# Strassen-style seven products, two 64-row tiles side by side, for the first two FFN products of two batches, with a new order of all steps

## The chip, the cores and the metric

The kernel runs on one core of one Trainium2 chip. The core has five engines with a queue of their own each: TensorE (PE, matrix products into the accumulator memory PSUM), VectorE (DVE), ScalarE (ACT), GpSimd (POOL), and SyncE (SP), which here only starts DMA transfers. The metric is the time of one execution in microseconds (us), as the device measures it; a profiled execution also has a span, from its first instruction to its last.

## The reference

A linear attention is followed by a feed-forward network (FFN) without a nonlinearity other than a product:

```python
def phi(x):                       # x: batch 4, heads 4, 1088 positions, 32 wide
    a = np.einsum('rd,bhsd->bhsr', S1, x)
    b = np.einsum('rd,bhsd->bhsr', S2, x)
    return np.einsum('bhsi,bhsj->bhsij', a, b).reshape(*x.shape[:-1], r * r)
...
num = np.einsum('bhsf,bhfd->bhsd', q_p, kv)
den = np.einsum('bhsf,bhf->bhs', q_p, z)[..., None] + 1e-06
...
# x: 4352 rows of 128, w1 and w2: 128x1024, w3: 1024x1024, w_out: 1024x128
a = x @ w1
b = x @ w2
h = a * b @ w3
return (h @ w_out).astype(np.float32)
```

All values are float32, S1, S2 and the weights reach the kernel as float64 words.

## The kernel before

**Stages.** The rows of the FFN are cut into nine groups: g0 to g7 have 512 rows each (two per batch), gr has the 256 rows that are left. The attention of a group ends in the tile xT (128 x 512, the row's 128 values down the partitions). The work in front of that (steps named k0 to k3, q0 to q6, qr, s) and the conversion of the weights from float64 words (w0 to w10, with c and m on ACT, j on DVE, a0 and a1 on POOL) is spread over the first two thirds. w3 and w_out are folded into one 1024x128 matrix w3o (f0 to f7).

**The FFN of one group.** For each of eight column blocks c there are four steps: `g.ca` (PE, x @ w1 block, line 1463), `g.cc` (ACT copies the result from PSUM, line 1468), `g.cb` (PE, x @ w2 block, line 1473) and `g.cm` (DVE multiplies the two, line 1479). `g.co` (PE, line 1486) then adds the block's product with w3o into the output bank. After the eighth, `g.oT` (DVE, line 1502) transposes the output and `g.st` has SP store it. Each of these PE steps is a float32 product of a 128x128 weight with 512 columns; the hardware runs it as two passes, each a weight load (LDWEIGHTS, in the profile's row PEld) and a MATMUL.

**Tiles of the PE array.** A product may be given a part of the array: `tile_position` and the sizes choose rows and columns. The kernel does this already for small products: ps_x (line 1423) and ps_ac (line 1310) use sixteen tiles of 32x32, ps_ab (line 665) eight of 64x32, ps_g (line 597) four of 128x32, and ps_x of the second group (line 1235) two of 128x64 with 512 columns each. None uses 64x128.

**Order.** There is no scheduler at run time. The string ORDER names every step once, and each engine executes its instructions in that order; the sets POOL and ACTS say which steps go to POOL or ACT instead of DVE. SLOTS deals out the buffers by hand, in order of use: eight PSUM banks (kind b), 13 tiles of 128x1024 (l), 32 of 128x512 (m) and so on. A step that reuses a buffer waits until its last reader is done. The loads wait further: no more than four large ones (UNDER_WAY) are under way at a time, in the order of SP's queue. `warm` steps multiply zeros while the PE has nothing else at the start.

In q_wide, for batches 2 and 3 (keys q4 and q6, 1024 rows at once), `x` leaves the attention's results in four PSUM banks and the steps `xT0` and `xT1` (line 1434) copy them with ACT into the xT tiles of two groups, g4 and g5, or g6 and g7.

Of the kernel before, what the change touches and what calls it, by code (L numbers as in the profile page):

```python
# [14 lines left out]
I32 = mybir.dt.int32  # L15
# [8 lines left out]
KIND = {"b": "out h kvz t wa wb", "l": "ph kp cv_m cv_c kh pT w3c w3T", "m": "t2 qT q2 s_hl xT ffa ab ay_C oT",  # L24
# [5 lines left out]
        "012345670452704612036071564164527526452430275310436027143627021423516041607354160735647256"  # L30
        "205137204637203512375163025713640271364072365724061562131760314053147531431431040431214201"
        "36034213602714356710243756047356473674671746025673523650247136504316031653416421460414376",
    "k_g": "0101",
    "l": "0123456789abc0127638954b0a12c357a09283b171427619c704a281b7c58307c2c397621530c2ab",
    "m": 
        "0123456789abcdefghijklmnopqrstuv35104297a8c6hdjgefqstko9mi3h6j1avb4s875pdo13a469j4bo21kd2v"
        "ib26c0mj8eshnti4fqba6vg1p5c9ku7r38otlbs6dqg2rhl6fn7gha1amgtvq8org7qrt4hmer1m6gndgs6n85h5m9"
        "360ubvokijtp",
    "q_m": "0101010",
    "raw": "012012020120120",  # L40
    "s": "012345671502364710523460731245630",
    "x": "012021021201",
}

WARM = [29, 2, 2, 9, 3, 2, 2, 3, 2, 1]
# [16 lines left out]
c.zeros c.ident s.four warm0 q0.load v0.zero k0.zero s.zero c.act s.load q0.tr k0.load0 k0.loadr k0.load1 s.words  # L62
k0.max0 k0.max1 c.mask kr0.load k0.tr1 kr0.tr k0.tr0 s.pair s.lead warm1 s.low s.sum s.rest s.T s.P k0.g k0.lead0
q0.max k0.rest0 s.tc warm2 s.R warm3 q1.tr kr0.kT q0.l2 s.Pc s.c q0.l1 k0.kT1 k0.gram0 s.blk s.blkh s.Pm q0.restT s.KS
q0.rm w1.load k0.lead1 warm4 q0.A0 q1.max k0.ab1 kr0.ab q0.C0 k0.abc1 q0.sma q0.sta k0.rest1 k0.kT0 k1.zero k0.kp1
k1.load s.Pp q1.l2 v0.load q0.C0t k0.gram1 k0.gram2 k0.gram3 k0.gram4 k0.Gm k0.Gt k0.Ga v0.loadr k1.loadr k0.ab0
kr1.load w0.load q0.sha k0.Gb k0.T0 w1.m warm5 q1.l1 k1.tr0 warm6 k1.tr1 q0.sla k0.Ta k0.N0 k0.abc0 warm7 k0.Gc w1.c
k0.kp0 q0.sca kr1.tr warm8 k2.zero kr0.abc k2.loadr k1.max k0.T1 k0.kv0 k0.kv3 k0.Na q0.al q0.phi0 k0.Tc kr1.kT
k1.lead0 k0.Nh q1.rm q0.A1 q0.pt0 k0.Tb k0.N1 kr0.kp q0.smy k0.Nb k0.Nf q0.sty q0.shy k0.kv1 k0.kv2 k0.kvr q0.C1
q0.phi1 q0.C1t q0.sly q0.p01 q1.C0 q0.pt1 q0.scy q0.p2 q0.p12 q0.dn q0.de q0.rc k0.kvm q1.load q0.pc0 q0.pc1 w9.load  # L70
k0.kzt k0.kz k2.load w1.j w1.a0 w1.a1 q1.C1 kr1.ab warm9 q1.Ct k1.kT0 q0.x1 q0.x0 k1.kT1 q1.A0 q0.xs0 q0.xs1 q0.xt0
q0.xc0 q0.xc1 k0.kvc q0.xT0 q0.xt1 q0.xT1 k1.ab q1.sm q1.st q1.sh k1.rest0 k0.kqt g0.6a g0.7a w0.m q1.sl w0.c g0.6c
g0.5a g0.4a q2.tr q1.sca q1.al q1.scy k1.gram0 k1.gram1 k1.gram2 k1.gram3 k1.gram4 q1.p01 q1.p2 q2.max q2.l2 w6.load
kh2.load w0.j kr1.abc g0.5c k2.max g0.7b g0.7c q1.p12 q1.dn k1.Gm q1.de s.AR k3.zero g0.6b w0.a0 k1.abt k1.Gt g0.0a
q1.rc g0.4c q1.bs k1.Ga k1.Gb k1.T0 k1.Gc k1.T1 q3.tr g0.7m g0.0c k1.Ta q1.phi g0.2a q1.pt1 k1.Tb k1.Tc k1.N0 k1.N1
k1.Na g0.5b w0.a1 g0.6m k1.Nr q1.pt0 q3.max q1.pc0 q2.l1 g0.1b g0.3a q3.l2 g0.1a g0.2c g0.4b q1.pc1 q1.x g0.1c
k2.lead0 k2.rest0 k2.gram0 k2.gram1 k2.gram2 k2.gram3 k0.kq q3.l1 k1.Nb k2.gram4 q2.rm s.RC g0.4m k2.kT0 k2.kT1 g0.5m
k2.Gm q2.A0 q2.C0 q2.C1 k2.Gt q3.rm g0.3c k2.Ga k2.Gb q2.Ct w9.c w6.m q1.xT g1.5a g1.5c g0.1m q2.At k1.kp0 g1.1a g1.1c
q1.restT k2.ab q2.sm k3.loadr w2.load w2.c k2.abt w9.m q2.st q2.sh q2.sl q3.A0 q3.C0 q3.C1 g0.0b q3.At q2.sc q3.Ct
g1.7b g1.2a q2.p01 q2.al q2.p2 g1.6a g1.4a g1.2c g1.4c k2.Gc q3.sm g0.0m v1.zero v1.load g1.3b g1.7a k1.kp1 q3.st  # L80
v1.loadr k3.load q2.load g1.7c q2.p12 q2.dn q3.sh k1.kv0 k1.kv2 k1.kv3 k1.kv1 k2.T0 k2.T1 k1.kvr q3.sl g1.5b q2.de
q3.sc q3.p01 q3.al q2.rc q2.bs q3.p2 k1.kvc k1.kqt k1.kq v2.zero w5.load k2.Ta k2.Tb g1.3a g1.6c g1.3c w9.j g0.3b
g1.2b w6.c g1.7m q3.p12 q2.phi0 k3.max g1.0a g1.1b kh3.load g1.3m g1.5m g1.2m g1.0c q2.pT0 g1.0b k2.Tc q2.x g0.3m
w9.a1 w5.m q2.xT0 k2.N0 k2.N1 w5.c g0.2b w9.a0 k2.Na w7.load k3.lead0 w2.j q3.dn g2.7a g2.7c w7.m w7.c k3.kT1 q4.tr
q3.de g1.1m g1.0m g2.2a g1.4b g2.4a g2.5a g2.5c w3.load k3.rest0 w5.j g1.4m k3.gram0 k3.gram1 k3.gram2 k3.gram3
k3.gram4 w6.j k3.Gm k3.Gt q3.rc k3.Ga k3.kT0 q3.bs k3.Gb g2.3a w5.a1 g2.2c w2.m q2.restT q4.max w7.j g2.7b g1.6b g2.6a
k3.Gc g2.1a g2.3c q4.l2 g2.4c w3.m g2.1c g2.6c g2.0a g2.0c k2.Nr g0.2m g1.6m g2.7m q3.phi0 kr1.kp q3.pT0 w2.a0 w2.a1
w6.a1 w6.a0 f6.t g2.5b g2.3b g2.3m g2.4b g2.0b k3.T0 k3.T1 g2.5m k2.Nb g2.4m g2.0m v2.load q3.x k3.ab k3.Ta k3.abt
f6.m q4.l1 q3.xT0 g3.2a g3.2c w3.c q4.rm q3.load g3.4a f6.o g3.0a g3.0c k3.Tb v3.zero f3.t f3.m f3.o k3.kp1 w5.a0 f2.t
k2.kp1 w3.j w3.a1 w4.load k3.Tc q4.A0 q4.C0 q4.C1 k3.N0 k3.N1 f2.m f2.o g3.4c w3.a0 w7.a0 w4.c w4.m q4.Ct q4.At w4.j  # L90
w4.a1 w7.a1 f0.t g2.2b q6.tr k0.Nr w10.load w10.m w10.c g2.2m f4.t g3.7a g3.0b g3.1a g3.6a g3.0m f0.m f0.o g2.6b w4.a0
q6.max w10.j g2.6m g3.1b v3.load k3.Na k3.Nr w8.load g3.5a g2.0o q3.restT k3.Nb k2.kp0 f4.m w8.c f4.o k3.kp0 f1.t
g3.6b q6.l2 g3.7c g3.5c g3.6c g3.6m g2.1b g2.4o g2.1m g3.3a g1.0o q6.l1 q4.sm q6.rm g3.7b g3.7m g3.4b g3.1c g3.1m
g3.4m f1.m k2.kv0 k2.kv3 v2.loadr k2.kv1 k2.kv2 k2.kvr k3.kv0 w8.m f1.o k3.kv1 k3.kv3 v3.loadr k3.kv2 k2.kvc k3.kvr
q6.A0 q6.C0 q6.C1 q4.st q6.At q6.Ct q4.sh g3.3c g0.0o g0.1o g1.1o g3.0o g1.6o k2.kqt w8.j w8.a0 w8.a1 f5.t g1.3o g0.2o
g1.4o g0.6o g0.3o qr.max g3.4o f5.m w10.a0 q4.sl q4.sc q4.p01 w10.a1 q4.al q4.p2 g2.6o k2.kq f5.o g1.5o g1.2o g3.3b
q4.p12 f7.t q6.sm g3.3m g3.2b g3.2m q4.dn qr.l2 qr.l1 qr.rm f7.m f7.o g3.3o k3.kvc k3.kqt k3.kq g3.1o g1.7o g3.6o
# [23 lines left out]
def make_steps(ctx, tc, q, k, v, S1, S2, moe_w1, moe_w2, moe_w3, moe_w_out, out):  # L121
# [1330 lines left out]
    def ffn(g, n, dst, halves=1):  # L1452
        w = n // halves
        for c in range(NC):
# [26 lines left out]
            if g != "r":  # L1481
                @step(f"g{g}.{c}o")
                def _(c=c):
                    if c == 0:
                        o_ps[g] = ps("out", [128, 512], "ps_o")
# [103 lines left out]
```

## Time and profile before

| | us |
|---|---|
| three runs | 252.36, 253.60, 256.84 |
| median | 253.60 |
| profiled execution: time | 253.12 |
| profiled execution: span | 251.3 |
| PE busy in the span | 245.4 |
| DVE busy | 151.1 |
| ACT busy | 104.7 |
| POOL busy | 87.2 |

The profile lists groups of instructions by line of the kernel with their number, their busy time together and the mean of one in ns. A MATMUL's own duration holds its way through the array, which overlaps the next one's start, so the distance from one start to the next is what counts; the chain of waits shows it, as it books each piece of time once. The granted TensorE clock is 1.0 all through. The DMA engines are busy for the first 100 us or so and then nearly idle but for the stores.

### The profile page before, as it was taken

The numbers are of one execution on the slowest core, as the hardware profiler recorded it, in microseconds if no ns is written. First come the engines' busy times: TensorE is split into PE (matmuls) and PEld (weight loads), VectorE is DVE, ScalarE is ACT, GpSimd is POOL, SyncE is SP. The second block draws the span as 40 slices with busy tenths as digits, with TensorE's granted clock in tenths as the row PEclk, the third lists the DMA queues.
The fourth block names the chain that finished last, engine by engine and source line by source line (L and its number), as shares of the span: only waits on it lengthen the run. The fifth ranks groups of instructions, "written<-read, shape, count | busy, mean of one in ns | idle before, by whom it ended". The sixth has DMA issues, their size and how long they took to land.

```text
span 251.3 us, 6192 instructions
## 1 busy us (share of the span) xinstructions
PE 245.4 (98%) x2582; PEld 136.8 (54%) x2582; DVE 151.1 (60%) x322; ACT 104.7 (42%) x210; POOL 87.2 (35%) x112
## 2 busy tenths in 40 slices
PE   8999989999999999999999999999999999999994
PEld 6887544655554676657466444454444445654554
DVE  2698997999799966674539557463523262332320
ACT  2999946755787337464011103433134112210000
POOL 4533966456649886620662550000010000000000
PEclk9999999999999999999999999999999999999999
DMA  7597988586788965000000000025000004000133
GB/s 203 170 244 223 247 183 185 126 261 174 170 196 227 230 178 113 0 4 3 0 3 0 3 0 0 1 36 92 0 0 0 3 4 80 0 3 0 21 63 63
DMA packets 32075, 22.02 MB, mean 88 GB/s; under 512 B 21296, under 2 KB 26672, under 8 KB 32048
## 3 DMA queue, kind: packets, MB, share of 16 engines
q1 hardware_dynamic: 31360, 21.05, 34.5%
q10 hardware_dynamic: 688, 0.59, 0.7%
q8 instruction: 20, 0.33, 0.6%
q14 instruction: 7, 0.06, 0.1%
HBM read 19.40 MB, written 2.23 MB: 86 GB/s over the span
## 4 chain that ended last, share of the span: by engine, by line
PE 88%; DMA 7%; SPq 2%; ACT 1%; DVE 0%; issue 0%
PE b_ps L1473 23%; PE ps_o L1486 22%; PE a_ps L1463 22%; PE ps_w3o L472 6%; DMA k<-in_k_dram 3%; PE idle_ps L220 3%; PE ps_x L1423 2%; PE ps_ac L1310 2%; DMA raw<-in_moe_w_dram 2%; PE ps_kv L707 2%; DMA kr<-in_k_dram 1%; PE ps_g L597 1%; PE ps_or L1493 1%; SPq L531 1%; ACT k_abs L172 0%; PE ps_N L850 0%
## 5 line engine op out<-in xcount | busy, mean ns | idle before, releaser
L1479 DVE TENSOR_TENSOR ab<-ffa,b_ps 128x512 f32<-128x512 f32 (+1 forms) x72 | 45.2, 647 | 53.9 <-PE b_ps L1473 26.6
L1468 ACT COPY ffa<-a_ps 128x512 f32<-128x512 f32 (+1 forms) x72 | 38.7, 567 | 78.1 <-PE a_ps L1463 70.9
L1463 PE MATMUL a_ps<-xT,w 128*128 128x512 f32 (+1 forms) x144 | 66.2, 574 | 0.4 <-DVE kabt L683 0.4
L1473 PE MATMUL b_ps<-xT,w 128*128 128x512 f32 (+1 forms) x144 | 66.3, 573 | 0.0
L1486 PE MATMUL ps_o<-ab,w3o 128*128 128x512 f32 x128 | 60.0, 594 | 0.0
L1463 PEld LDWEIGHTS a_ps<-xT,w 128*128 128x128 f32 x144 | 26.5, 190 | 30.8 <-issue 22.6
L1473 PEld LDWEIGHTS b_ps<-xT,w 128*128 128x128 f32 x144 | 26.5, 190 | 28.5 <-issue 23.1
L1486 PEld LDWEIGHTS ps_o<-ab,w3o 128*128 128x128 f32 x128 | 23.8, 190 | 25.1 <-issue 23.9
L439 POOL TENSOR_TENSOR w3c<-w3c,cv_m 128x512 int32<-128x512 int32 x16 | 20.1, 1270 | 15.8 <-DVE w3c L433 13.3
L472 PEld LDWEIGHTS ps_w3o<-wo,w3T 128*128 128x128 f32 x128 | 15.4, 192 | 3.3 <-issue 2.0
L1405 POOL TENSOR_TENSOR ph<-s_al,s_bs 128x1024 f32<-128x1024 f32 (+1 forms) x5 | 9.9, 1975 | 19.5 <-DVE s_bs L1395 13.2
L472 PE MATMUL ps_w3o<-wo,w3T 128*128 128x128 f32 x128 | 15.8, 276 | 0.0
L420 ACT ACTIVATE cv_m<-raw 128x1024 int32<-128x1024 uint32 x11 | 12.9, 1182 | 4.0 <-PE ps_w3o L472 3.5
L466 DVE STREAM_TRANSPOSE w3T<-w3c 128x1024 f32<-128x1024 f32 x8 | 9.9, 1240 | 6.7 <-POOL w3c L439 4.5
L228 ACT ACTIVATE cv_c<-raw 128x1024 f32<-128x1024 f32 x11 | 13.0, 1179 | 0.0
L615 POOL TENSOR_TENSOR kp<-kabt 128x1024 f32<-128x1024 f32 x6 | 12.5, 2084 | 1.0 <-DVE kabt L683 1.0
L589 POOL TENSOR_TENSOR kk<-k,kk 128x1152 f32<-128x1152 f32 (+1 forms) x4 | 9.7, 2434 | 5.6 <-DVE kk L179 4.4
L220 PE MATMUL idle_ps<-zeros 128*128 128x256 bf16 x55 | 10.6, 349 | 1.0 <-DVE zeros L194 1.0
L476 ACT COPY w3o<-ps_w3o 128x128 f32<-128x128 f32 x8 | 2.1, 262 | 20.2 <-PE ps_w3o L472 20.2
L1434 ACT COPY xT<-ps_x 128x128 f32<-128x128 f32 (+2 forms) x20 | 4.7, 322 | 13.4 <-PE ps_x L1423 13.4
L1372 POOL TENSOR_TENSOR s_pr<-s_al,s_hl 128x128 f32<-128x128 f32 (+2 forms) x4 | 2.4, 589 | 20.6 <-DVE s_al L1362 20.6
L1413 DVE STREAM_TRANSPOSE pT<-ph 128x1024 f32<-128x1024 f32 (+1 forms) x7 | 8.2, 1167 | 1.0 <-POOL ph L1405 0.8
(260 smaller groups left out, 300.4 us busy)
## 6 DMA issues: line engine op xcount, KB each, us to landing
raw<-in_moe_w_dram SPq DMA_DIRECT2D x32, 256.0 KB, 5.1
qh<-in_q_dram SPq DMA_DIRECT2D x4, 544.0 KB, 3.9
out_dram<-oT SPq DMA_DIRECT2D x33, 64.0 KB, 1.9
raw<-in_moe_w_dram SPq DMA_DIRECT2D x4, 512.0 KB, 5.4
k<-in_k_dram SPq DMA_DIRECT2D x3, 512.0 KB, 5.1
v<-in_v_dram SPq DMA_DIRECT2D x2, 512.0 KB, 4.1
kh<-in_k_dram SPq DMA_DIRECT2D x8, 128.0 KB, 3.2
raw<-in_moe_w_out_dram SPq DMA_DIRECT2D x4, 256.0 KB, 5.7
```

The costliest lines, as they stand in the source:

```text
L220: pe.matmul(t, zeros, bview(zeros, [[0, 2], [1, 128]]), start=True, stop=True)
L228: act.activation(dst, hi.bitcast(F32), ACT.Prelu, scale=2.0 ** -112, alpha=-2.0 ** 32)
L420: act.mul(x["m"], words(0).bitcast(U32), 2.0 ** -29)
L439: pool.tensor_tensor(d, d, x["m"][:, i * 512:(i + 1) * 512], ALU.add)
L466: dve.transpose(w3T[ko].rearrange("p s (i r) -> p s i r", r=32), bview(w3c[ko], [[32, NC], [256, 4], [1, 32]]))
L472: pe.matmul(t["o"], w3T[ko][:, c], wo[:, c], start=c == 0, stop=c == NC - 1)
L615: eng.tensor_mul(dst, bview(av, [list(av.ap[1]), list(av.ap[2]), [0, r]]), bview(bv, [list(bv.ap[1]), [0, r], list(bv.ap[2])]))
L1463: pe.matmul(x["a"][:, :w], w_of(0, c), xT[g][:, c0:c0 + w], start=True, stop=True)
L1468: act.copy(x["s"][:, :w], x["a"][:, :w])
L1473: pe.matmul(x["b"][:, :w], w_of(1, c), xT[g][:, c0:c0 + w], start=True, stop=True)
L1479: dve.tensor_mul(ab_sb[g, c][:, c0:c0 + w], x["s"][:, :w], x["b"][:, :w])
L1486: pe.matmul(o_ps[g], w3o[:, c], ab_sb[g, c], start=c == 0, stop=c == NC - 1)
```

## The change

The two first FFN products of batches 2 and 3 are computed as block products. With x of one batch cut into two row halves (groups g and g+1) and two halves of 64 of the inner dimension, and a weight cut likewise into two halves of 64 rows and two halves of 512 columns, a 2x2 by 2x2 block product takes seven products of blocks in place of eight (the Winograd form of Strassen's method). Each is a 64x128 tile with 512 columns. The product of w1 (u=0, "a") sits in rows 0 to 63 of the array, that of w2 (u=1, "b") in rows 64 to 127; they are separate steps in ORDER.

```diff
+    def seven(g):
+        mv = {}
+        own = {1: (0, 0), 2: (0, 1), 4: (1, 1)}
+        ...
+        @step(f"h{g}.s1")
+        def _():
+            mv[5] = sb("xd", [128, 512], name="xd")
+            on(f"h{g}.s1").tensor_add(mv[5], xd[g, 1][0], xd[g, 1][1])
+        ...
+        for i in range(NC // 2):
+            both = {}
+            for u in range(2):
+                ...
+                def prod(j, bank, new, i=i, u=u, x=x, n=n):
+                    @step(n(j))
+                    def _():
+                        if new:
+                            x[bank] = ps("h", [128, 512], "ps_" + bank)
+                        pe.matmul(x[bank], stat(j, u)[:, i * 128:(i + 1) * 128], rows(j, u), start=new, stop=True,
+                                  tile_position=(u * 64, 0), skip_group_check=True)
+                def take(y, bank, k, n=n, x=x):
+                    ...
+                        act.copy(x[k], x[bank])
+                def plus(y, bank, k, n=n, x=x):
+                    ...
+                        dve.tensor_add(x[k], x[k], x[bank])
+                prod(1, "X", True)
+                take("c", "X", 11)
+                prod(5, "Y", True)
+                take("d", "Y", 22)
+                prod(6, "X", False)
+                take("e", "X", 12)
+                prod(3, "Y", False)
+                plus("f", "Y", 12)
+                prod(7, "X", False)
+                plus("g", "X", 22)
+                prod(2, "Z", True)
+                plus("h", "Z", 11)
+                prod(4, "X", False)
+                if u == 0:
+                    take("i", "X", 21)
+            for k, (t, c) in {11: (0, 0), 12: (0, 4), 22: (1, 4)}.items():
+                @step(f"h{g}.{i}m{k}")
+                ...
+                    on(f"h{g}.{i}m{k}").tensor_mul(both[0][k], both[0][k], both[1][k])
+            @step(f"h{g}.{i}m21")
+            ...
+                dve.tensor_mul(both[0][21], both[0][21], both[1]["X"])
     def ffn(g, n, dst, halves=1):
         w = n // halves
-        for c in range(NC):
+        whole = g != "r" and g >= 4
+        for c in range(0 if whole else NC):
```

`s1` to `s4` are four sums or differences of this size. So a bank X takes four products one after the other, and an engine reads it after each: ACT, ACT, DVE, and last ACT (for u=0) or DVE. For each i (four per pair of groups) that makes 14 products, 7 copies by ACT, 6 sums by DVE and 4 multiplications; 13 of the 32 multiplications are in the set POOL. The products with w3o take the blocks in the order 0, 4, 1, 5, 2, 6, 3, 7.

What goes with it:

- `v.s`, `v.t` (ACT, two copies of 64x512) and `v.1` to `v.4` (POOL, eight subtractions of 64x512) make the sums of weight blocks.
- `xT0` to `xT3` of q4 and q6 write the tiles xd, split by inner half: each step four copies of 64x256, on ACT for xT0 and xT2, on DVE for xT1 and xT3.
- In q4 and q6 the rows of x are scaled by powers of two: `na`, `nb` (peaks, DVE), `nm`, `nn` (multiplications), `nr`, `ne` (small, DVE), and `ns` (17 small instructions, POOL), which makes the factors that undo it. `oS` multiplies the transposed output by them (POOL for g4 and g6, DVE for g5 and g7).

```diff
+            if whole:
+                @step(f"g{g}.oS")
+                def _():
+                    y = oT[0].rearrange("p (t d) -> p t d", d=32)
+                    on(f"g{g}.oS").tensor_mul(y, y, bview(scale[g], [[1, 16], [0, 32]]))
```

ORDER, SLOTS, POOL and WARM are new throughout. The PE's order from the first of the new products to the end is, with a and b for a 64x128 product of either kind, x for a ps_x of 32x32 tiles, O for a product with w3o (line 1486 before), g and r for gr's products:

```
abbaaba x abbaababaab x babaababbaabbbaaababab OOO abbaababbaababababab
OO g OOOOOO g OO g OOO g bababbaaabbbaaabbbaababab g O g
baabbbaaababbbaaabbababaabab OOO gggg OOOO g OOOOOOOO ggggg rrrrrrrrrrrrrrrr
```

From the first FFN product on, the shape of the tiles changes 38 times along PE's queue before, and 48 times after. In SP's queue the load of w0 (half of w1 and w2) stands behind w1, k1, v0, kr1 before; after, it stands behind these and the loads of kh2 (four), k1's rest and q1:

```diff
-k1.load s.Pp q1.l2 v0.load q0.C0t k0.gram1 k0.gram2 k0.gram3 k0.gram4 k0.Gm k0.Gt k0.Ga v0.loadr k1.loadr k0.ab0
-kr1.load w0.load q0.sha k0.Gb k0.T0 w1.m warm5 q1.l1 k1.tr0 warm6 k1.tr1 q0.sla k0.Ta k0.N0 k0.abc0 warm7 k0.Gc w1.c
...
+k0.kv0 k0.kv3 k0.T1 kr0.kp k0.Na kr1.tr q0.al k0.Nh k0.Tb q1.l1 k2.loadr kh2.load k0.Tc k1.kT1 k1.kT0 q0.phi0 q1.A0
+q0.A1 q0.smy k0.N1 k0.Nb k0.kv1 k0.kv2 k0.kvr q0.phi1 k0.kvm k0.Nf q0.pt0 q0.sty q0.shy q0.C1 k0.kvc k1.loadr q0.pc0
+q1.rm k0.kzt q0.pt1 k1.max kr1.kT s.AR q0.p01 q0.sly q0.C1t q0.scy q1.load q0.p2 q0.p12 k0.kz w0.load k2.load k0.kqt
...
+kr1.ab q1.Ct k1.abt k1.lead0 w0.c w1.a0 s.RC k1.rest0 w0.j q3.tr g0.4a g0.7a g0.5a w0.m g0.6a k1.gram0 k1.gram1
+k1.gram2 k1.gram3 k1.gram4 w6.load w9.load w2.load g0.5c w1.a1 q1.sm q1.st q2.tr k2.kT1 g0.4b q3.max g0.7c k1.Gm k1.Gt
+q1.sh g0.6c k0.kq k2.max w0.a1 w0.a0 g0.4c g0.2a g0.1b k1.Ga q1.sl q1.scy q1.sca k1.Gb g0.4m k1.Gc kr1.abc k1.T0
```

274 lines of the change are left out of this document (195 added, 79 removed).

## The prediction

> **What bounds the kernel now.** I read the page's busy table first, then the windows for three stages, then the chain of waits, and last the groups of lines.
>
> ```profile
> span 251.3 us, 6192 instructions
> PE 245.4 (98%) x2582; PEld 136.8 (54%) x2582; DVE 151.1 (60%) x322; ACT 104.7 (42%) x210; POOL 87.2 (35%) x112
> ```
>
> ```profile
> 26.80:40.00 13.20, 11.93 (x209) 6.20 (x208) 11.36 (x30) 7.76 (x17) 10.19 (x10) 1.00 0.86 197
> 40.00:150.00 110.00, 109.98 (x1411) 61.88 (x1410) 83.42 (x163) 52.98 (x96) 62.52 (x55) 1.00 0.42 104
> 150.00:248.20 98.20, 97.92 (x460) 48.68 (x458) 37.69 (x71) 22.55 (x49) 2.35 (x3) 1.00 0.13 22
> ```
>
> The window columns are the stretch, then busy time of PE, PEld, DVE, ACT and POOL, the granted clock, the DMA share and GB/s. From the first FFN product (26.8 us) to the last one PE has no gap worth naming except 1.27 us before 40. In the last stage, where the change is, DVE is busy for 37.69 of 98.20 us, ACT for 22.55, POOL for 2.35. But busy is not yet full: what one pass of a product costs is read from the chain of waits (start, length, what).
>
> ```profile
> 41.43 1.72 PE a_ps L1463 x4
> ...
> 44.08 1.01 PE ps_x L1235 x4
> 45.08 1.82 PE ps_g L597 x88
> ...
> 48.08 1.91 PE a_ps L1463 x4
> ...
> 122.85 5.15 PE ps_o L1486 x12
> ...
> 244.57 3.36 PE ps_or L1493 x30
> 247.96 0.29 DVE oT L1513
> ```
>
> Twelve passes of 512 columns take 5.15 us, 0.429 each, and four take 1.72. The same four take 1.91 behind the ps_ac piece, which uses small tiles: a change of tile shape costs 0.19. So the end is PE's sum of passes, plus a price for each change of shape, plus the tail of stores behind 248.25.
>
> **The products.** Removed are 4 groups x 8 blocks x 2 products x 2 passes = 128 passes x 0.429 = 54.9 us. Added are 2 pairs x 4 blocks x 2 sides x 7 = 112 products of 64x128 tiles. Whether two of them run at once, no row of 64x128 shows. The nearest is ps_x at line 1235: two tiles of 128x64 side by side, four passes of the same 512 columns in 1.01 us where the full array needs 1.72. Two rounds of 0.429 are 0.86; the 0.15 left over is one entry and exit. I take it that two row tiles overlap in the same way. How many rounds that makes I counted on PE's order: a change of shape lets both sides run out, so each of the six stretches lasts as long as its longer side, 4, 6, 11, 10, 13 and 14 products, 58 in all where 56 would be ideal. That holds if PE may start a b that stands behind two or three a's. If it may not, the same walk gives 62.
>
> ```profile
> L597 PE MATMUL ps_g<-kk 128*32 128x64 f32 x288 | 7.5, 224 | 0.3 <-POOL kk L589 0.2
> L597 PE MATMUL ps_g<-k,kk 128*32 128x32 f32 x288 | 7.2, 194 | 0.0
> ```
>
> ps_g decides for 58: it puts two products in a row on each of its four tiles. At 0.429 us for 512 columns, 288 passes of 64 columns and 288 of 32 stream for 15.4 + 7.7 = 23 us, and all of it is done in about 7.5, three tiles at a time. PE does look past a busy tile. So 58 x 2 x 0.429 = 49.8 us; saved: **5.1 us** (bounds 1.7 and 5.1).
>
> The loads of weights double to two for each round.
>
> ```profile
> L1486 PEld LDWEIGHTS ps_o<-ab,w3o 128*128 128x128 f32 x128 | 23.8, 190 | 25.1 <-issue 23.9
> ```
>
> A load takes 190 ns, and passes on one array still follow every 0.429 us, so a load is hidden behind the pass before it on the same rows. The Trainium skill (TensorE: Matmul & The Clock Gate, Part 3, The mechanism) says that a load overlaps matmuls under way only where the row group differs, which speaks against this change: each side would wait for its own loads. The trace differs, by the 0.429, and I go by the trace.
>
> **Changes of shape.** 48 in place of 38 on PE's queue from the first FFN product on: 10 x 0.19 = **1.9 us** lost. From the 0.15 of an entry and exit together it would be 0.8; I take 0.19, since it is of a full-width load.
>
> **Work on the other engines.**
>
> ```profile
> L1479 DVE TENSOR_TENSOR ab<-ffa,b_ps 128x512 f32<-128x512 f32 (+1 forms) x72 | 45.2, 647 | 53.9 <-PE b_ps L1473 26.6
> L1468 ACT COPY ffa<-a_ps 128x512 f32<-128x512 f32 (+1 forms) x72 | 38.7, 567 | 78.1 <-PE a_ps L1463 70.9
> L439 POOL TENSOR_TENSOR w3c<-w3c,cv_m 128x512 int32<-128x512 int32 x16 | 20.1, 1270 | 15.8 <-DVE w3c L433 13.3
> ```
>
> ```profile
> L1434 ACT COPY xT<-ps_x x20: 267/296/402, 66.6 to 206.7; 128x128 f32<-128x128 f32 x8, 128x256 f32<-128x256 f32 x8, 128x64 f32<-128x64 f32 x4
> L1502 DVE STREAM_TRANSPOSE oT<-ps_o x8: 698/714/718, 148.9 to 244.6; 128x512 f32<-128x512 f32 x8
> ```
>
> DVE in the last stage: 37.69, plus 48 sums x 0.647 = 31.1, minus 13 multiplications that go to POOL (8.4), plus eight copies of q6 at about 0.296 (2.4), plus three s and two oS at 0.647 (3.2): 66 of some 95 us. ACT: 22.55 + 24 more copies x 0.567 + 2.4 = 39. POOL: 2.35 + 13 x 1.27 + two oS and five s at 1.27 = 28, and the small copies of `ns` (priced at 0.3 each from the shortest xT copies, 32 of them 10). All lie beside PE. The v and n steps of q4 come before 150 us, where POOL has 47 of 110 us free; eight subtractions at 1.27 are 10. The densest stretch is the one of 13 products: PE 13 x 0.857 = 11.1 us, DVE 12 sums, a multiplication, an oS, gr.5m (at most 0.647) and a transpose, 15 x 0.647 + 0.714 = 10.4. That is 94%, and there the cover is thin: DVE's queue runs in order, so a late sum holds all sums behind it, and the PE product that reuses its bank.
>
> This is the new kind of wait: a bank X gets four products, and between two of them an ACT copy (0.567) or a DVE sum (0.647) must end. Eight banks and two sides leave other products to run meanwhile. In the kernel before such waits are small:
>
> ```profile
> PEld a_ps L1463 <- ACT ffa L1468: 2.0, 5, 0.6
> PEld ps_g L597 <- POOL kk L589: 1.9, 2, 1.1
> ...
> PEld a_ps L1463 <- POOL w L439: 1.2, 1, 1.2
> ```
>
> Five waits of weight loads for the copy make 2.0 us, most of it hidden by the pass under way. Bounds for the new waits: nothing, or one DVE sum for each of the eight blocks, 8 x 0.647 = 5.2. I take 0.6, near the lower end, as that row is.
>
> **What is moved.** At the start w0's load goes behind q1's, which waited for PE:
>
> ```profile
> 15.30 1.08 SPq L395 DMA_DIRECT2D raw<-in_moe_w_dram  x2
> ...
> 21.50 0.33 SPq L913 DMA_DIRECT2D qh<-in_q_dram  x1
> ```
>
> ```profile
> 19.59 1.25 ACT L176 ACTIVATE kk<-k,k_g 128x1152 f32<-128x1152 f32 x1
> ...
> 26.84 3.66 PE L1463 MATMUL a_ps<-xT,w 128*128 128x512 f32 x8
> ```
>
> ```profile
> raw<-in_moe_w_dram SPq DMA_DIRECT2D x4, 512.0 KB, 5.4
> ...
> L420 ACT ACTIVATE cv_m<-raw 128x1024 int32<-128x1024 uint32 x11 | 12.9, 1182 | 4.0 <-PE ps_w3o L472 3.5
> L228 ACT ACTIVATE cv_c<-raw 128x1024 f32<-128x1024 f32 x11 | 13.0, 1179 | 0.0
> ```
>
> If q1 is still issued at 21.5, w0 follows at 21.9 (15.30 before), lands 5.4 later at 27.3, and needs two ACT conversions (2.4) and two POOL additions (2.5): 32.2, or 34.7 if ACT's k1.lead0, now in front of it, delays it by two passes of 1.25, as the row of the same operation shows. PE has other work to about 33: behind 26.84 four products of w1 (3.4), k1's gram (1.8, from the ps_g piece of the chain) and one b (0.86). The 1.2 us wait for w in the row above becomes 0 to 1.7; I take no difference. The rest of the head is only shuffled; the first product's time may shift by a microsecond either way, which I leave to the range.
>
> At the end DVE has, behind g7's last block, two transposes, an oS and six gr multiplications: 2.1 + 6 x 0.647 at most = 6.0, PE meanwhile five gr products (2.1) and ps_or (3.36): 0 to 0.5, taken as nothing. The last store follows as before.
>
> **Sum.** The profiled execution took 253.12, its span 251.3 with 1.8 around it; the median of the three runs, 253.6, lies 0.5 above. 253.1 - 5.1 + 1.9 + 0.6 = **250.5 us**.
>
> **Rivals.**
> - *The new order also recovers the head.* If the waits for kk (1.9) and w (1.2) go and no new ones come: 249.9 - 3.1 = 246.8. For it: these are the only idle stretches left, and the order is new throughout. Against it: both hang on loads and conversions of which w0's comes later now.
> - *The banks' chain becomes the bound.* One sum's length lost per block: 249.9 + 5.2 = 255.1. For it: 94% DVE in one stretch. Against it: 69% over the stage. It decides once DVE's share in a stretch passes PE's.
> - *Side by side costs each pair what line 1235 cost once (slower).* If the 0.15 above the two rounds is not entry and exit but paid by every pair of products: 58 x 0.15 = 8.7, 249.9 + 8.7 = 258.6. It beats the saving from 0.055 per pair on. Against it: the 0.15 is smaller than one change of shape. The same page of the Trainium skill (Part 3, Measured speedup) gives 3.07 for four row tiles instead of 4; by that factor 49.8 would be 65 us, an estimate, and the result 265. No run here shows row tiles of that size.
> - *Loads do not hide in a half array.* Each side pays 58 x 2 x 0.190 = 22.0: 271.9. This is what the overlap rule would do; against it stands 0.429 per pass with 0.190 loads.
>
> **Chances.** Forecast 0.59 (its own range 248.8 with the cheap changes of shape and no waits, to 252.0), head 0.16, chain 0.13, pairs 0.09, loads 0.03. The range 246.8 to 258.6 reaches from the head to the pairs. Two per cent, about what a measurement tells, is 248.1 and 258.2. Faster: 0.16 + 0.02 from the forecast's edge = 0.18. Slower: 0.09 + 0.03 + 0.02 from a worse chain = 0.14. Within: 0.68.
>
> **What would show it.** Two rows of 64x128 passes that start within a few ns and follow on each side every 0.43 us, PE about 98% busy, and a stage from the first new product to the last ps_or some 3 us shorter. A spacing of 0.5 or 0.62 shows the third or fourth rival. Waits of PE or PEld for the sums or copies of the new banks above 2 us show the second. A first FFN product far from 26.8 us shows that the head, not the products, made the difference.

## The result, and the profile after

| | before | after |
|---|---|---|
| runs shown (us) | 252.36, 253.05, 253.60, 256.84 | 259.58, 261.18, 262.10, 262.60 |
| median | 253.32 | 261.64 |
| ratio after/before, 95% interval | | 1.033, 1.0245 to 1.0416 |
| profiled execution: time, span | 253.12, 251.3 | 259.58, 257.8 |
| first FFN product starts | 26.84 | 26.74 |
| last product of ps_or starts | 247.65 | 253.68 |

The changed kernel is 3.3% slower. The profiled execution of it is its fastest: there the granted TensorE clock was 1.0 throughout, in the three others it averaged 0.983 to 0.990, and they took 1.6 to 3.0 us more; the last section comes back to this. Some executions of a kernel take over 1.5% longer than its fastest; the medians in this document hold all executions, the ratios leave these out.

The busy table of the page and the windows (stretch, then busy time of PE, PEld, DVE, ACT and POOL, granted clock, DMA share, GB/s) answer to those of before; the windows are cut at the first new product, 157.7 us:

```profile
span 257.8 us, 6599 instructions
...
PE 246.1 (95%) x2681; PEld 139.6 (54%) x2681; DVE 187.5 (73%) x388; ACT 123.9 (48%) x244; POOL 126.7 (49%) x178
```

```profile
26.80:40.00 13.20, 10.43 (x170) 5.25 (x170) 9.37 (x25) 8.67 (x18) 5.35 (x8) 1.00 0.88 227
40.00:150.00 110.00, 107.05 (x1503) 61.21 (x1502) 95.34 (x196) 58.08 (x104) 75.08 (x80) 1.00 0.43 105
150.00:157.70 7.70, 7.70 (x20) 3.21 (x18) 7.53 (x10) 0.00 (x0) 2.99 (x4) 1.00 0.00 1
157.70:254.30 96.60, 95.21 (x481) 49.15 (x480) 57.67 (x101) 37.48 (x78) 30.34 (x40) 1.00 0.14 23
```

PE, which was idle for 1.27 us between 26.8 and 40 and for 0.02 from there to 150, is now idle for 2.77 and 2.95. That is in front of the new products. PE's waits (engine, line, what it waited for: total, times, longest) say for what:

```profile
PE ps_g L608 <- issue: 2.5, 2, 2.0
PE b_ps L1664 <- ACT ffa L1659: 1.4, 1, 1.4
...
PE a_ps L1654 <- POOL w L450: 0.9, 1, 0.9
PE ps_ac L1314 <- POOL AR L903: 0.8, 1, 0.8
PE ps_X L1601 <- ACT hc L1608: 0.6, 1, 0.6
```

The second and third are w0. The chain of waits there (start, length, what) shows that the load took 8.8 us, where 5.4 was the median before; ACT's conversion, in order, held the copies ffa behind it, and POOL's additions came last:

```profile
22.65 8.77 DMA raw<-in_moe_w_dram
...
31.50 1.16 ACT cv_c L239
32.66 1.05 ACT cv_m L431
...
33.78 2.50 POOL w L450 x2
...
36.33 0.70 PE a_ps L1654
```

The fourth is a small product of batch 3 that waits for `k3.Nr` on POOL, in whose queue `v.1` (two subtractions) now stands in front. The first and longest wait has no releaser: "issue" is time in which the engine waited for nothing that the profile shows. PE's timeline (start, length, what, count, and in brackets the idle time before) shows it in the middle of the small products of k2's gram:

```profile
46.79 0.22 PE L608 MATMUL ps_g<-kk 128*32 128x64 f32 x1
46.80 0.23 PE L608 MATMUL ps_g<-k,kk 128*32 128x32 f32 x2
49.07 0.19 PE L608 MATMUL ps_g<-k,kk 128*32 128x32 f32 x1 [2.05 <-issue]
```

All products around it are of one step on data that is there. What arrives just then is seen in the page's table of DMA queues (packets, MB, share): PE's instructions themselves.

```profile
q8 instruction: 21, 0.34, 0.6%
```

PE has 5424 records here (weight loads, passes, sequencer), so one of the 21 packets of 16 KB goes with some 258 of them; in the kernel before it is 20 packets for 5209. In the trace one of these packets starts at 46.65 and takes 1.10 us; 1.33 us after it landed PE goes on. The shorter stand of ps_g, 0.67 us at 31.3, ends 1.46 us after another. Counted in order from 0, PE goes on there with instructions 1729 and 1217, which are 512 apart, two chunks of 256. That made the theory that most experiments below test: **PE had run out of instructions.**

The new products do run two side by side. The chain in a stretch that has as many a's as b's:

```profile
183.35 1.06 PE ps_X L1601 x4
184.41 0.42 PE ps_Z L1601
184.84 0.01 PE ps_X L1601
184.84 0.42 PE ps_Z L1601
185.26 0.01 PE ps_X L1601
185.27 0.86 PE ps_Y L1601 x4
```

Two passes of 512 columns start 0.01 us apart or less, and the next two follow 0.42 later; four take 0.86, half of 1.72 on the full array. The stretches as a whole, windows again:

```profile
157.74:161.55 3.81, 3.81 (x15) 1.37 (x14) 3.34 (x9) 2.28 (x5) 2.57 (x3) 1.00 0.40 62
163.90:169.86 5.96, 5.88 (x28) 2.70 (x23) 5.50 (x12) 5.57 (x13) 5.07 (x15) 1.00 0.28 46
170.64:180.51 9.87, 9.87 (x50) 4.92 (x44) 7.74 (x13) 5.71 (x13) 4.09 (x5) 1.00 0.01 2
183.28:192.15 8.87, 8.87 (x42) 4.30 (x41) 5.94 (x9) 3.91 (x7) 3.77 (x3) 1.00 0.00 0
205.23:217.09 11.86, 11.86 (x52) 6.67 (x51) 8.63 (x15) 6.05 (x11) 1.64 (x2) 1.00 0.21 35
219.31:232.80 13.49, 12.92 (x55) 5.96 (x54) 5.74 (x9) 7.26 (x14) 5.04 (x5) 1.00 0.05 8
sum 53.86, PE 53.20 PEld 25.92 DVE 36.91 ACT 30.78 POOL 22.19; mean PE 8.87 PEld 4.32 DVE 6.15 ACT 5.13 POOL 3.70
```

53.86 us, where 49.8 were forecast. If each pass counts its columns at full rate (0.429 us for 512 on the whole array), PE's passes from the first FFN product on are some 205 us before and 198 after: (128 - 112) x 0.429 = 6.9 were taken off the array. But in the stage behind 150 us, 3.3 us were lost beside the passes before, and 9.8 after. So this stage ends up with some 0.4 us gained, and the stages in front lose some 6.5. Behind the last product of ps_or 0.4 us more are lost (4.1 us to the end of the span, 3.7 before).

### The profile page after: what moved, and what is told of

It is laid out like the page before. It is cut to its first block, busy times and chain, and to the rows that moved or that the text cites. A ratio compares the mean times of both kernels' runs of the same rounds, so it can differ in the third digit from the quotient of the medians.

```text
span 257.8 us, 6599 instructions
## 1 busy us (share of the span) xinstructions
PE 246.1 (95%) x2681; PEld 139.6 (54%) x2681; DVE 187.5 (73%) x388; ACT 123.9 (48%) x244; POOL 126.7 (49%) x178
## 4 chain that ended last, share of the span: by engine, by line
PE 80%; DVE 5%; POOL 5%; DMA 3%; ACT 2%; issue 2%; SPq 0%; ACTq 0%; DVEq 0%; POOLq 0%
PE ps_o L1689 21%; PE ps_X L1601 11%; PE b_ps L1664 10%; PE a_ps L1654 10%; PE ps_Y L1601 6%; PE idle_ps L231 4%; DMA raw<-in_moe_w_dram 3%; PE ps_Z L1601 3%; PE ps_g L608 2%; PE ps_x L1476 2%; PE ps_ac L1323 2%; PE ps_w3o L483 2%; PE ps_or L1678 1%; PE ps_kv L718 1%; ACT xd L1489 1%
## 5 line engine op out<-in xcount | busy, mean ns | idle before, releaser
L1601 PE MATMUL ps_X<-xd,wv 64*128 64x512 f32 x112 | 41.0, 605 | 0.6 <-ACT hc L1608 0.6
L1608 ACT COPY hc<-ps_X 128x512 f32<-128x512 f32 x40 | 22.5, 591 | 37.1 <-PE ps_X L1601 33.3
L1659 ACT COPY ffa<-a_ps 128x512 f32<-128x512 f32 (+1 forms) x40 | 21.1, 548 | 34.8 <-PE a_ps L1654 32.5
L1664 PE MATMUL b_ps<-xT,w 128*128 128x512 f32 (+1 forms) x80 | 36.4, 559 | 1.5 <-ACT ffa L1659 1.4
L1654 PE MATMUL a_ps<-xT,w 128*128 128x512 f32 (+1 forms) x80 | 35.6, 557 | 0.9 <-POOL w L450 0.9
L1635 POOL TENSOR_TENSOR hc<-hc 128x512 f32<-128x512 f32 x13 | 16.2, 1273 | 29.6 <-DVE hc L1613 29.6
L1689 PE MATMUL ps_o<-ab,w3o 128*128 128x512 f32 x64 | 29.4, 597 | 0.0
L1689 PE MATMUL ps_o<-hc,w3o 128*128 128x512 f32 x64 | 29.3, 599 | 0.0
L1670 DVE TENSOR_TENSOR ab<-ffa,b_ps 128x512 f32<-128x512 f32 (+1 forms) x40 | 23.9, 619 | 7.5 <-PE b_ps L1664 7.5
L1601 PE MATMUL ps_Y<-xd,wv 64*128 64x512 f32 x48 | 20.6, 603 | 0.1
```

The costliest lines, as they stand in the source:

```text
L1601: pe.matmul(x[bank], stat(j, u)[:, i * 128:(i + 1) * 128], rows(j, u), start=new, stop=True, tile_position=(u * 64, 0), skip_group_check=True)
L1608: act.copy(x[k], x[bank])
L1635: on(f"h{g}.{i}m{k}").tensor_mul(both[0][k], both[0][k], both[1][k])
L1654: pe.matmul(x["a"][:, :w], w_of(0, c), xT[g][:, c0:c0 + w], start=True, stop=True)
L1659: act.copy(x["s"][:, :w], x["a"][:, :w])
L1664: pe.matmul(x["b"][:, :w], w_of(1, c), xT[g][:, c0:c0 + w], start=True, stop=True)
```

## Experiments

The theory "order" says that the loss comes from what the new order of all steps does in front of the new products; the rival "products", that the products and their side work cost more than they save. Ratios are to the kernel before in the same runs, since its median moved between 253.5 and 255.9 from one set of runs to the next. Where steps were moved, buffers were dealt out anew only where needed.

**Half the change each.** head_of_before:

```diff
 ORDER, POOL, WARM
-    the changed kernel's, up to q1.x
+    those of the kernel before, up to k2.kT1 (46 us); then what is left, in the changed kernel's order
```

> The changed kernel with the steps of the first 46 us in the order, the POOL set and the warm-up of the kernel before; everything behind them, the seven products too, in the changed kernel's order. Theory 'order' (the loss of the changed kernel comes mostly from idle stretches of PE that the new order makes in front of the new products: 2.9 us more lost between 26.7 and 50 us, 3.5 more from 50 to 150): the 2.9 come back, 261.6 - 2.9 = 258.7. Rival 'products' (the seven products and their side work cost more than they save, and idle stretches in front only move): no gain, 261 to 262.

Measured 262.96 us, 1.029 (1.017 to 1.041): no gain. It settles nothing: at the seam a DVE step of q3 runs for 4.6 us, until 53 us, beside two multiplications of POOL (1.9 us each; in the changed kernel's trace the same step takes 2.35), PE stands 2.3 us for what is behind it on DVE, and the granted clock is at half behind that (shown in the last section).

eight_in_new_order:

```diff
-    xd, v, n, s steps; 2 x 4 x 14 products of 64x128
+    g4 to g7 with 64 ordinary products, from q4.bs on in the order of the kernel before
```

> The eight ordinary products in place of the seven: the changed kernel's order up to q4.bs (127 us there) without the v and n steps, then the rest in the order of the kernel before. Theory 'order': the losses of the head and the middle stay without the seven products, 253.3 + 2.9 + 0.8 + about 1.5 = 258.5. Rival 'products': about 253.3, as the kernel before.

Measured 263.72, 1.036 (1.028 to 1.045). Without a single new product the new order is as slow as the changed kernel. That speaks for "order", though one stretch of 2.7 us at 129 us, behind work of POOL, belongs to the seam, and the clock was at half for 6.8 us from 34.6. PE stood at instructions 1217 and 1729 here too, 1.23 and 1.40 us.

**The waits that the trace names.** w0_early and w0_early_v1_late:

```diff
-q1.load q0.p2 q0.p12 k0.kz w0.load k2.load
+q1.load q0.p2 q0.p12 k0.kz k2.load
-kr1.load kr0.abc
+kr1.load w0.load kr0.abc
```

> The changed kernel with the one step w0.load moved forward, to right behind kr1.load, as in the kernel before. If the late landing of w0 makes PE's gaps at 32.8 (1.55 us) and 35.3 (1.07 us): 261.6 - 2.6 = 259.0, and those two gaps are gone in the profile; the gaps at 31.3 (0.65) and 46.9 (2.2), which end with no releaser, stay. Rival: w0's conversion is late for another reason (ACT's queue in front of it), no change, 261.6.

```diff
-qr.max v.1 k2.kp0
+qr.max k2.kp0
-k3.Nr q4.p2
+k3.Nr v.1 q4.p2
```

> As w0_early, and the step v.1 (POOL, two subtractions of 64x512) moved behind k3.Nr in POOL's queue. If the gap of 0.98 us at 115.4 (a product waits for AR, whose step stood behind v.1) is real loss: 1.0 less than w0_early, about 258.0. Rival: the q4 chain behind it is what the stage waits for, same as w0_early.

Measured 260.64, 1.026 (1.018 to 1.034), and 259.56, 1.022 (1.015 to 1.029). The gaps named do go, but less than their length is won with the first: its first FFN product starts at 30.0 us, since PE stood 2.5 us at instruction 705 and then ran at half clock from 22 to 25 us. The stands at ps_g stayed, both in w0_early and the longer one in w0_early_v1_late, 2.30 us.

**Where PE's instructions are cut.** after_phase and before_phase add instructions to the warm-up at the very start and leave everything else alone:

```diff
+            for _ in range(26 if name == "warm0" else 0):      # before_phase: 77
+                pe.matmul(t[:, :16], zeros, zeros[:, :16], start=True, stop=True)
-WARM = [30, ...                                              # before_phase: 29
+WARM = [24, ...                                              # before_phase: 10
```

> The changed kernel with the first warm-up of 30 products of zeros (256 columns) replaced by 24 of them and 26 of 16 columns: about as long, but 40 PE instructions more (a weight load and a pass each). Theory 'instruction fetch': PE's instructions come in chunks of 256 (16 KB, one fetch of the instruction queue each), and PE stands where a chunk runs out before the next has come; in three kernels of this order it stood at the same instructions, the 1217th and the 1729th, 512 apart. 40 more in front move the chunks' borders out of the small products of ps_g: the two stretches at 31.3 (0.65) and 46.9 us (2.2) go, 261.6 - 2.9 = 258.7, and less if the granted clock then also stays at 1.0. Rival (memory or semaphores hold ps_g, or the fetch is late whatever the border): both stretches stay at ps_g, 261 to 262.

> The kernel before with the first warm-up of 29 products of zeros replaced by 10 of them and 77 of 16 columns, 116 PE instructions more, nothing else. Theory 'instruction fetch': from the times of PE's instructions, a chunk of 256 needs about 4.3 us, and with this shift the chunks' borders fall so that ps_g at 32 and 47 us, and chunks at 117 and 170 us, come up to 2.8, 2.7, 2.4 and 1.7 us late: 4 to 9 us slower, 258 to 262. Rival: where the borders lie does not matter, within 1 us of the kernel before, 253 to 254.5.

Measured: after_phase 257.23, 1.0155 (1.0115 to 1.0196), from 1.033, and neither stand is left in its trace. (Its wait for the copies ffa is shorter too, 0.3 us for 1.4.) before_phase 260.85, 1.032 (1.026 to 1.039): with 116 more instructions of zeros the kernel before is as slow as the changed one. The theory had the places wrong, and that the size came out was luck: of the 6.8 us that the profiled execution lost, 4.2 are stands, 1.24, 1.30 and 1.64 us in other small products, at instructions 705, 961 and 1985. Much of the rest lies in the head, where the nine warm-up products of `warm3` take 2.10 us for 1.16 before.

repaired and seven_on_before were the next try at both theories:

```diff
 repaired: w0_early_v1_late
+with the warm-up of after_phase
 seven_on_before: head_of_before
-with its seam at k2.kT1
+with its seam at q6.A0 (116 us)
```

> The changed kernel with all three repairs: w0.load early, v.1 behind k3.Nr, and the 40 instructions of after_phase. If the losses in front of the new products are these: 259.6 (w0_early_v1_late) - 2.3 (the one stretch left at ps_g there) - 1 to 2 of granted clock = 255 to 257. Rival: the losses only move, 259 or more.

> The kernel before's order, POOL set and warm-up up to q6.A0 (116 us there), then the rest in the changed kernel's order with the seven products and the scaling. Theory 'order' (the seven products by themselves save little but do save): the stage behind 150 us loses 0.75 us less than before, so 253.3 - 0.75 + up to 1.5 for the seam = 252.5 to 254. Rival 'products': 258 or more.

Measured 258.13, 1.022 (1.015 to 1.030), and 273.19, 1.077 (1.070 to 1.084). The repairs do not add up: repaired has only 1.4 us of idle PE from its first FFN product to the last of ps_or, but that starts at 30.6 us, behind a wait of 2.6 us and 3.4 us at half clock: in its chain of waits w0's load (7.9 us) now stands in front of one of k (2.4 us), and ACT's work on that k in front of the copies that lead to the product. seven_on_before is a miss that tells nothing of the products: its seam puts a fold's transpose behind work of DVE and POOL, and its longest waits are there.

```profile
PE ps_w3o L478 <- DVE w3T L472: 6.5, 1, 6.5
PE b_ps L1659 <- ACT ffa L1654: 2.5, 1, 2.5
PE b_ps L1659 <- DVE ay_C L1335: 2.2, 1, 2.2
```

**A control, POOL, the scaling, and the order of the new products.** before_phase_256 puts 147 for the 77 small products. after_phase_v1 is after_phase with `v.1` behind `k3.Nr`. no_scaling drops 18 steps from it. balanced has the 366 steps from the first new product to the end in an order that a search with a small model of that stage found.

> As before_phase, but with 147 instead of 77 small products of zeros in the first warm-up: 256 PE instructions more than the kernel before in place of 116, one whole chunk, so that every border lies where it lay. Theory 'instruction fetch': the loss of before_phase goes, 253 to 255. Rival (the small products warm PE up worse than the 29 full ones, and that is what made before_phase slow): about as before_phase, 259 to 261.

> after_phase with v.1 moved behind k3.Nr on POOL (w0.load stays late). If the stretch of 0.95 us at 112 (a product waits for AR) is real loss: 257.2 - 0.95 = 256.3. Rival: the chain behind it sets the pace, no change, 257.2.

> after_phase_v1 without the scaling by powers of two (the steps na, nb, nm, nr, ne, nn, ns of q4 and q6 and oS of g4 to g7 are left out). The prediction costed this work at nothing, since it lies beside PE: then 256.3 as after_phase_v1, within 0.5. Rival: the steps between bs and phi0 of q4 and q6 lengthen the chain that the new products wait for, and DVE and POOL lack the time in the last stage: 1 to 2.5 us less, 254 to 255.

> after_phase_v1 with all steps from the first 64x128 product to the end in another order (same steps, buffers dealt out anew): products of the two halves alternate more evenly, and the sums and copies come sooner. A model of that stage, which gives the measured times of after_phase within 1 us, puts the end 5.6 us earlier. Theory (the stage of the new products loses 9.6 us, of which about 3 to waits and one-sided rounds, because of its order, not by nature): 256.3 minus 3 to 5, 251.5 to 253.5. Rival (each pair of products has a price that order does not change): 255.5 or more.

before_phase_256: 258.50, 1.011 (0.999 to 1.022), no clear control: in its profile no border stops PE from the first FFN product on, but that starts only at 33.7 us. Its head is slow: the nine warm-up products take 2.10 us for 1.16, PE stands 2.09 us at instruction 705, and the clock is at half for 3.4 us from 22.1. after_phase_v1: 254.77, 1.0102 (1.0029 to 1.0175); the gap is gone. no_scaling: 255.85, 1.0106 (1.0038 to 1.0174), the same within these intervals. In its profile PE stood 1.58 us at instruction 1729 (0.55 in after_phase_v1's) and waited for w0, so the totals don't price the scaling. The stage from the first new product to the last of ps_or does; first after_phase_v1, then no_scaling:

```profile
151.37:247.13 95.76, 94.80 (x481) 49.07 (x480) 57.17 (x100) 37.29 (x78) 30.29 (x40) 1.00 0.13 22
155.29:250.09 94.80, 94.11 (x480) 48.92 (x480) 54.27 (x94) 37.34 (x78) 22.66 (x19) 1.00 0.12 21
```

Without the scaling it is 1.0 us shorter; it is 95.7 to 95.9 in the traces of the changed kernel, after_phase, w0_early and seven_48, which have the same steps there.

balanced: 261.31, 1.024 (1.015 to 1.033), against the theory, but it is no clean test of the order of the products. Its stage is as long as before, 96.1 us. Of the 7.5 us between the profiled executions of balanced and after_phase_v1, 3.8 lie in front of the first new product, where the order is nearly the same (it waits for w0 again), and 3.4 behind the last of ps_or: the eight transfers of a group's store, which take SP 4.2 us, are issued only from 251.5 us on. Its stretches of new products take 55.3 us instead of 53.8. Two of the five show what the model lacked, as windows:

```profile
157.66:170.58 12.92, 11.35 (x47) 5.49 (x43) 8.32 (x18) 8.99 (x19) 5.04 (x5) 1.00 0.47 77
171.43:188.77 17.34, 17.34 (x75) 12.32 (x75) 15.49 (x24) 8.79 (x19) 6.90 (x5) 1.00 0.00 1
```

In the second, 74 passes that would take 15.9 us in pairs take 17.3 with PE never idle: the two halves run one after the other where one has work and the other waits. In the first PE waited 1.6 us for a copy.

**The control again, and the products alone.** border_116 and border_256 cut the kernel before's first warm-up into more products with as many columns together, so it is as long and as warm. seven_48 is the changed kernel with `v.1` late and the warm-up cut likewise; eight_48 has the same head and ordinary products.

```diff
-    29 products of 256 columns        # seven_48, eight_48: 30 of 256
+    87 of 86 (border_116)   157 of 48 (border_256)   54 of 142 (seven_48, eight_48)
```

> The kernel before with its first warm-up of 29 products of zeros of 256 columns cut into 87 of 86 columns: as many columns, so as long and as warm, but 116 PE instructions more. Theory 'borders': PE stands at the borders that before_phase had (1.2, 1.3, 1.6 and 0.3 us in its trace, 4.4 together), 253.4 + 4.4 = 258, 256 to 260. Rival 'warm-up' (before_phase was slow since small products warm less): as the kernel before, 253 to 254.5.

> The same with 157 products of 48 columns: 256 PE instructions more, a whole chunk, so every border lies where it lay. Theory 'borders': as the kernel before, 253 to 254.5. Rival (any more instructions in front cost time): as border_116 or slower.

> The changed kernel with v.1 behind k3.Nr and its first warm-up cut into 54 products of 142 columns (30 of 256 before): 48 PE instructions more, the shift for which the times of PE's instructions in the changed kernel's trace give no late chunk. Theory 'borders': the rest of the stand at the 1729th instruction (0.55 us in after_phase_v1) goes too, 254.8 - 0.5 = 254.3. Rival: no better than after_phase_v1, 254.8 or more.

> seven_48 with the eight ordinary products: the same order, POOL set and warm-up up to the first new product (157 us in the changed kernel), without the v, n and s steps, and the rest in the order of the kernel before. What is lost against seven_48 is what the seven products with all side work are worth. The prediction's terms: 5.1 - 1.9 - 0.6 = 2.6 us slower than seven_48, 256.9. By the two traces' stage behind 150 us: 0.75 slower, 255. Rival (their side work also costs the middle): faster than seven_48, 252 to 254.

border_116: 257.32, 1.0119 (1.0036 to 1.0202). border_256: 253.72, 0.9992 (0.9947 to 1.0037). 116 instructions more cost 3 us, 256 more cost nothing that these intervals show. PE's waits, first in border_116 and then in border_256:

```profile
PE ps_ac L1311 <- issue: 2.6, 2, 1.4
```

```profile
PE idle_ps L221 <- DVE zeros L194: 1.0, 1, 1.0
PE a_ps L1464 <- DVE kabt L684: 0.4, 1, 0.4
PE ps_krt L758 <- DMA kr<-in_k_dram: 0.3, 1, 0.3
PE ps_g L598 <- POOL kk L590: 0.2, 1, 0.2
```

In border_256 no wait on "issue" is left. (The profiled execution of border_116 also waits 1.3 us for a load of kr in the head, which is not of the borders.) The stands of PE, counted by its instructions from 0 in the traces:

| kernel | instruction (stand in us, start behind the landing of a chunk) |
|---|---|
| changed | 1217 (0.67, 1.46), 1729 (2.24, 1.33) |
| w0_early | 705 (2.48, 1.59), 1217 (0.96, 1.55), 1729 (1.69, 1.39) |
| w0_early_v1_late | 705 (3.04, 1.44), 1729 (2.30, 1.44) |
| eight_in_new_order | 1217 (1.23, 1.45), 1729 (1.40, 1.26) |
| before_phase | 705 (1.24, 1.57), 961 (1.30, 1.25), 1985 (1.64, 1.43) |
| before_phase_256 | 705 (2.09, 1.73) |
| no_scaling | 1729 (1.58, 1.44) |
| border_116 | 961 (0.48, 1.47), 1985 (1.68, 1.19), 4033 (1.61, 1.45) |
| eight_48 | 1217 (0.57, 1.52) |
| seven_w0 (below) | 1217 (2.32, 1.37) |

Every number is 193 plus a multiple of 256, in ten kernels and at several different steps, and PE goes on 1.2 to 1.7 us after a packet has landed. That a chunk's border stops PE is shown.

seven_48: 255.03, 1.0046 (1.0007 to 1.0085). eight_48: 255.02, 1.0027 (0.9982 to 1.0072). With the head alike and little or no stand at a border (none in seven_48's trace, 0.57 us in eight_48's), seven products are worth as much as eight: the ratios differ by 0.5 us, with intervals of about 1 us to either side of each, so the forecast gain of 2.6 us is not there, and a gain or a loss of 1 us is left open.

**What is left: w0 once more.** seven_loads moves two loads, seven_w0 one:

```diff
 seven_loads
-k2.loadr kh2.load ... k1.loadr ... q1.load ... w0.load k2.load
+... k1.loadr ... q1.load ... w0.load k2.loadr kh2.load k2.load
 seven_w0
-q0.scy q1.load q0.p2 q0.p12 k0.kz w0.load k2.load
+q0.scy w0.load q1.load q0.p2 q0.p12 k0.kz k2.load
```

> seven_48 with the loads k2.loadr and kh2.load moved behind w0.load in SP's queue, so that k1's rest, q1 and w0 come some 2 us earlier and k2's later (first needed at 35 us). Theory: w0's late landing is what is left of the loss in the head: the stretches of 1.1 and 1.1 us at 31 and 33 us go and the first FFN product stays at 26 us, 255.0 - 2.2 = 252.8, level with the kernel before. Rival (k2's loads then come late instead, or SP's limit of four loads delays w0 as before): 254.5 to 256.

> seven_48 with w0.load in front of q1.load in SP's queue instead of behind it. q1.load's wait for its buffer then no longer holds w0, which is issued some 2 us earlier (18.6 for 20.6 us). Theory: w0's late issue behind that wait is what is left in the head: the stretches of 1.1 and 1.1 us at 31 and 33 us go, 255.0 - 2.2 = 252.8. Rival (the limit of four loads under way, or their bandwidth, sets the landing, and q1 then comes late): 254.5 to 256.

seven_loads: 258.48, 1.020 (1.016 to 1.024), slower; PE now waits 3.5 us for ACT (kvc) at 62 us. And w0 came no earlier: SP's own waits show that q1's load in front of it waits for its buffer.

```profile
SPq L920 <- PE ps_kv L721: 6.1, 1, 6.1
```

seven_w0: 254.78, 1.0047 (1.0000 to 1.0094), as seven_48. Both waits for w0 are gone from its trace, but PE stood at a border again, at instruction 1217, in ps_g:

```profile
PE ps_g L604 <- issue: 2.1, 1, 2.1
PE ps_ab L672 <- DVE ay_C L1336: 0.2, 1, 0.2
```

The border lies where it lay in seven_48, whose trace has no stand there, and in PE's order it comes ahead of the two waits for w0. What differed is the packet: it started 7.45 us after PE had entered the chunk from instruction 961, and 2.10 us after it in seven_48. So the place of a border does not by itself decide what it costs, and what holds the packet back is not shown. No version beats the kernel before; seven_48 and seven_w0 come within 0.5% of it.

## Why the prediction was wrong

**Where the 11 us lie.** Forecast were 250.5, measured 261.6. In the profiled executions the stage behind 150 us gained some 0.4 us in place of 5.1 - 1.9 - 0.6 = 2.6; the stages between the first FFN product and that one lost some 6.5 where nothing was forecast; 0.4 are at the end. Of the 6.5, the stands are 2.9, the waits for w0 2.6 (1.2 before) and the wait for `k3.Nr` 1.0. The 2 us that remain go with the lower clock of the executions that weren't profiled.

**The step that failed is "What is moved":** "The rest of the head is only shuffled; the first product's time may shift by a microsecond either way". The first FFN product did start where it had, at 26.7 us; the cost lay behind it. The sum has a price for each product, copy and load, and none for where PE's instruction chunks end. The kernel before has its borders where they cost nothing: none of its stands lies at one. The new order moved others of the small products onto them, and PE stood 2.9 us for instructions in the profiled execution. Shifting the borders alone, with no step moved, took the ratio from 1.033 to 1.0155, 4.4 us by the medians; that holds the clock of the unprofiled runs and some of the wait for w0, which became shorter.

**w0's late load, "I take no difference".** Its own upper bound was 1.7 us in place of 1.2. The row gave 5.4 us for the landing, the trace shows 8.8, and the two waits were 1.55 and 1.07 us as gaps between passes. Here the mechanism was right (ACT's conversion late, POOL's additions last) and the landing was mis-sized. What its repair would be worth stays open: in w0_early and seven_w0 PE stood at a border instead.

**"The v and n steps of q4 come before 150 us, where POOL has 47 of 110 us free."** Free on average, but POOL's queue runs in order: `v.1` (two subtractions) stood in front of `k3.Nr`, for which a PE product waits; 0.98 us of idle PE. The scaling, costed at nothing ("All lie beside PE"), takes 1.0 us of the stage of the new products (no_scaling): the wait of a ps_x piece for DVE between the first two stretches (0.72 us from one start to the next) is gone without it.

**The products.** That two overlap, that loads hide and that the 0.15 us is paid once per stretch was right, and with it the third and fourth rival fall: weight loads of 64x128 take 186 ns, and pairs follow every 0.43 us. The overlap rule of the Trainium skill (TensorE: Matmul & The Clock Gate, Part 3, The mechanism) would not forbid that, since the two halves lie on different rows, but it would have a load wait for the pass before it on its own rows; the trace shows no such wait in the stretch from 183.3. The term of 49.8 us was mis-sized: the stretches took 53.86. Of the 4.1 between, 1.2 are entries and exits of the six stretches, which the sum books under changes of shape; 1.6 are waits inside the stretches, where 0.6 were forecast; the rest of 1.3 are one and a half rounds in which only one side had work. Outside them, the ps_x piece between the first two stretches takes 2.35 us for 0.85 of passes. Together these took nearly all of the saving: seven_48 and eight_48 differ by less than their intervals. Whether another order of the new products would bring it back stays open; balanced did not shorten the stage.

**The rivals.** "The new order also recovers the head" was wrong in sign. "The banks' chain becomes the bound" named a real wait (0.73 us at 226.6, PE for a copy of hc), but all waits in the stretches come to 1.6 us, a small part of the loss. The rival that came true, the head gets worse since instructions come late, was not on the list.

## What to carry to other kernels

Where hundreds of small products follow one another, ask whether the engine's instructions can arrive as fast as it executes them, and look for idle time that ends with no releaser just after a packet of the instruction queue. A gain or a loss of 1 to 2% after a reordering may be nothing but these borders: before judging such a change, shift the borders with a few idle instructions at the start, with a whole chunk as the control, and profile more than one such version, since the same border cost nothing in seven_48 and 2.3 us in seven_w0. And test an arithmetic saving with the rest of the order held still, as seven_48 and eight_48 do, before crediting or blaming it.

## What was not expected of the hardware

**PE's instruction supply.** In the changed kernel's trace PE enters the chunk from instruction 1473 at 44.65 us; the packet that brings the next one starts at 46.65, takes 1.10, and instruction 1729 starts at 49.07. So this chunk took 4.4 us, and the small products of ps_g had used it up in 2.2. How long after the entry the packet starts differs much: 2.00 us here and 1.36 in w0_early's trace for this chunk, 4.50 and 4.86 for the one from instruction 961. Why it starts so late stays open.

**The clock.** Idle time of little over 2 us can be followed by half clock. In w0_early_v1_late PE stands 3.04 us up to 23.08 (instruction 705) and 2.30 us up to 50.34 (instruction 1729), both at a border; windows show the granted clock in the third column from the right:

```profile
23.44:26.84 3.40, 3.40 (x62) 2.48 (x59) 2.04 (x7) 2.00 (x5) 0.59 (x2) 0.50 0.37 107
26.90:47.30 20.40, 20.40 (x368) 11.69 (x370) 18.36 (x49) 16.30 (x35) 12.01 (x16) 1.00 0.86 217
47.35:50.70 3.35, 1.24 (x102) 1.13 (x88) 3.20 (x5) 1.88 (x4) 3.35 (x3) 1.00 0.03 5
50.75:54.15 3.40, 3.40 (x81) 1.39 (x77) 0.00 (x0) 1.27 (x2) 1.04 (x1) 0.50 0.51 173
54.20:60.00 5.80, 5.80 (x118) 2.89 (x98) 5.24 (x21) 4.67 (x7) 2.03 (x4) 1.00 0.69 198
```

Each stand is followed by 3.4 us at half clock, 1.7 us lost where PE is the bound. In head_of_before PE stands for 2.33 us from 51.4, and, two passes later, 0.5 us more up to 55.38:

```profile
48.00:52.00 4.00, 3.56 (x116) 1.88 (x103) 4.00 (x2) 2.07 (x3) 4.00 (x4) 1.00 0.60 206
52.00:56.00 4.00, 1.74 (x12) 0.87 (x20) 3.97 (x13) 1.11 (x2) 0.52 (x1) 0.88 1.04 306
56.00:60.00 4.00, 4.00 (x89) 1.99 (x74) 3.36 (x13) 4.00 (x5) 2.60 (x4) 0.50 0.46 124
60.00:64.00 4.00, 4.00 (x9) 1.67 (x7) 3.18 (x10) 1.07 (x4) 1.49 (x2) 0.77 0.97 244
```

The three windows from 52 to 64 come to some 6.8 us at half clock, 3.4 us lost where PE is the bound. The Trainium skill (TensorE: Matmul & The Clock Gate, Part 1, What's actually happening) states that a free-running window of about 3.4 us decides, and that the clock drops after a window of idleness. The lengths of the slow stretches, about one such window and about two, agree, and in w0_early_v1_late the two begin 27.3 us apart, eight such windows; here 2.30 us of idle time were enough, and 2.24 in the profiled execution of the changed kernel were not. A mean of 0.987 over 260 us, as in one run of the changed kernel that wasn't profiled, is 6.8 us at half clock. That the stands at the borders set it off in those runs, as in the trace of w0_early_v1_late, is likely, but they have no trace.
